# A last batch finished chunk by chunk, and a first attention moved ahead of another batch's transform

## The chip, the cores and the metric

The kernel runs on one core of one Trainium2 chip. The metric is device time in microseconds (us). The traces show five engines of the core: TensorE (PE, matrix products; PEld is its weight load), VectorE (DVE), ScalarE (ACT), GpSimd (POOL) and SyncE (SP, which here only issues transfers). The profile's DMA share is a mean over 16 DMA engines. In this kernel PE writes its results to four PSUM tiles of 128 x 2 x 512 (the two halves are called banks here), and DVE and ACT copy results out of them: 128x512 in 0.69 us on DVE and 0.59 on ACT in the trace of before.

## The reference

```python
def _attn_ref(q, k, v, g_norm):                       # (8, 8, 576, 64) each
    kv = np.einsum('bhsd,bhse->bhde', k, v)
    out = np.einsum('bhsd,bhde->bhse', q, kv)
    rms = np.sqrt(np.mean(out * out, axis=-1, keepdims=True) + 1e-06)
    return (out / rms * g_norm)

def _moe_ref(x, w_proj, filter_fft, w_out):           # x: (8, 576, 512)
    proj = x @ w_proj                                  # 512 -> 3 x 512
    x1, x2, x3 = ...                                   # the three thirds
    X2 = np.fft.rfft(x2, n=S, axis=1)
    H = np.fft.rfft(filter_fft, n=S, axis=0)[None]
    x2_conv = np.fft.irfft(X2 * H, n=S, axis=1)
    return (x1 * x2_conv * x3) @ w_out
```

The output of the attention, its heads side by side, is x of the second function. Everything is float32 outside.

## The kernel before

Both transforms are matrix products with tables of sines. Batches are pipelined: while batch b goes through its transform (`fft`), its gates (`proj13`) and its inverse (`inv`), the attention of batch b + 1 runs (`att_o`, `att_r`, `att_x`), and then its fold (`fold`, the symmetric and antisymmetric parts of x that the projection `proj2` takes). The library that builds the program orders each engine's instructions itself, by readiness and by the order in which they are written; `keep_in_program_order` pins an instruction behind the one written before it on its engine.

```python
    def att_o(b, j):
        ...
        op = ps_tile("ps_o")
        for h in range(2):
            nc.tensor.matmul(op[:, h, 0:TH], kvblk[b % 2][:, j], ...)
        nc.scalar.activation(out=s['sq']..., in_=op[:, :, 0:TH], func=AF.Square)
        if b == 0:
            nc.vector.tensor_scalar_mul(out=o_, in0=op[:, :, 0:TH], scalar1=g_col)
        else:
            nc.scalar.activation(out=o_, in_=op[:, :, 0:TH], func=AF.Copy, scale=g_col)

    def fft(b, g):              # g < 2: two DVE products and a POOL sum; g == 2: one DVE product
        ...
            nc.vector.tensor_mul(out=t_[:n, 0], in0=xp[:n], in1=HH[:n, g, 1:3])
            nc.vector.tensor_mul(out=t_[:n, 1], in0=xp[:n], in1=HH[:n, g, 0:2])
            nc.gpsimd.tensor_add(out=Y[:n, 2 * g:2 * g + 2], in0=t_[:n, :, 0], in1=t_[:n, :, 1])

    def o_rows(b, *blks):       # a block of 64 columns of yg is 64 rows of the output, three apart
        t0 = [SB * (x // 3) + x % 3 for x in blks]
        two = [[(t0[1] - t0[0]) * DM, 2]] if len(t0) == 2 else []
        return bass.AP(tensor=out.tensor, offset=..., ap=[[3 * DM, 64]] + two + [[1, DM]])

    def last(b):
        po = [ps_tile("ps_out") for _ in range(3)]      # five chunks in three PSUM tiles
        ...
        for dc in range(NDC):
            inv(b, (dc,))
            if dc:
                part(dc - 1)                            # a quarter of every chunk
        part(NDC - 1)
        for c in range(NSC):
            ...                                         # copy: ACT for even c, DVE for odd
            for i in range(2):
                (nc.scalar if i else nc.sync).dma_start(out=o_rows(bb, blk), in_=ot[64 * i:64 * i + 64, 0])

    # batch 0's stage in the main loop
            att_o(1, 0); fft(0, 1); att_o(1, 1); att_r(1, 0); fft(0, 0); att_r(1, 1)
            att_x(1, 0); fold(1, 0); att_o(1, 2); proj13(0, 2); att_o(1, 3); att_r(1, 2)
            fft(0, 2); att_r(1, 3); att_x(1, 1); fold(1, 1); proj13(0, 3)
    # later, for every b: outp(b - 1, ...), then last(b) for the last batch, else inv(b, ...)
```

## Time and profile before

| | before |
|---|---|
| time, median of the first 3 runs | 255.63 us (254.88 to 257.65) |
| span of the profiled execution | 252.9 us |
| PE, DVE, ACT, POOL busy | 222.7, 195.1, 153.3, 89.7 us |
| row "43.40 to 61.70": PE idle | 5.2 us |
| row "230.90 to 253.00": PE idle | 10.1 us |
| last copy out of PSUM ends | 249.1 us |

A line of a timeline gives the start, the length, engine, source line, operation, output and input, and in brackets the engine's idle time before it with what ended it. The lines themselves stand in the prediction. The clock in a table by stretches is the one that PE was granted, 1.00 at full speed; the DMA share is the mean busy share of the 16 DMA engines. A run is marked slow when it takes over 1.5% more than the fastest of the same kernel. This line of the page gives the number of output transfers of 256 KB, and the median time from issue to landing:

```profile
out_dram<-ot SPq DMA_DIRECT2D x28, 256.0 KB, 3.6
```

### The profile page before, as it was taken

The numbers are of one execution on the slowest core, as the hardware profiler recorded it, in microseconds if no ns is written. First come the engines' busy times: TensorE is split into PE (matmuls) and PEld (weight loads), VectorE is DVE, ScalarE is ACT, GpSimd is POOL, SyncE is SP. The second block draws the span as 40 slices with busy tenths as digits, with TensorE's granted clock in tenths as the row PEclk, the third lists the DMA queues.
The fourth block names the chain that finished last, engine by engine and source line by source line (L and its number), as shares of the span: only waits on it lengthen the run. The fifth ranks groups of instructions, "written<-read, shape, count | busy, mean of one in ns | idle before, by whom it ended". The sixth has DMA issues, their size and how long they took to land.

```text
span 252.9 us, 4825 instructions
## 1 busy us (share of the span) xinstructions
PE 222.7 (88%) x1927; PEld 132.3 (52%) x1927; DVE 195.1 (77%) x354; ACT 153.3 (61%) x230; POOL 89.7 (35%) x101
## 2 busy tenths in 40 slices
PE   0377997787999999999999999999999999999760
PEld 0343453453665566655665566547664765466420
DVE  6669747799797969795998699769987997696441
ACT  2764336991689468945894689566956696522311
POOL 7964970670491049102920292003300330042000
PEclk9999999999999999999999999999999999999995
DMA  6999999993297529752994199420023003400506
GB/s 69 167 202 251 202 196 191 193 136 43 19 180 85 158 26 181 87 160 54 160 119 115 56 162 118 117 95 1 0 66 103 3 0 75 135 0 3 166 20 187
DMA packets 45623, 27.17 MB, mean 107 GB/s; under 512 B 22274, under 2 KB 40706, under 8 KB 45602
## 3 DMA queue, kind: packets, MB, share of 16 engines
q0 software_dynamic: 40160, 17.44, 55.1%
q1 hardware_dynamic: 5042, 8.78, 12.2%
q10 hardware_dynamic: 400, 0.66, 0.7%
q8 instruction: 15, 0.25, 0.4%
q14 instruction: 6, 0.05, 0.1%
HBM read 33.69 MB, written 9.44 MB: 171 GB/s over the span
## 4 chain that ended last, share of the span: by engine, by line
PE 69%; ACT 13%; DVE 9%; issue 3%; DMA 2%; POOL 2%; ACTq 1%; POOLq 0%; DVEq 0%
PE ps_x L432 19%; PE ps_out L481 10%; PE ps_x L383 6%; PE ps_invo L456 4%; PE ps_inve L456 4%; PE ps_qT L248 3%; ACT lr L284 3%; PE ps_x L389 3%; PE ps_x L374 3%; PE ps_r L283 2%; ACT osb L272 2%; ACT sq L267 2%; DMA vm<-in_v_dram 2%; PE ps_kv L223 2%; PE ps_o L266 2%
## 5 line engine op out<-in xcount | busy, mean ns | idle before, releaser
L432 PE MATMUL ps_x<-x,wp 128*128 128x288 bf16 x512 | 67.8, 286 | 0.7
L415 POOL TENSOR_TENSOR Y<-tpw 128x1024 bf16<-128x1024 f32 (+1 forms) x16 | 37.9, 2366 | 66.3 <-PE ps_r L283 40.7
L432 PEld LDWEIGHTS <-wp 128*128 128x128 bf16 x512 | 49.7, 98 | 15.5 <-issue 2.9
L70 POOL DMA_DIRECT2D km<-in_k_dram x9 | 7.9, 878 | 64.4 <-PE ps_qT L248 58.4
L267 ACT ACTIVATE sq<-ps_o 128x576 bf16<-128x576 f32 x32 | 20.7, 653 | 13.4 <-PE ps_o L266 13.4
L438 DVE TENSOR_TENSOR g<-ps_x,x 128x576 bf16<-128x576 f32 x32 | 24.0, 751 | 5.3 <-PE ps_x L432 3.5
L284 ACT ACTIVATE lr<-ps_r,bias_eps 128x576 f32<-128x576 f32 x32 | 23.5, 751 | 6.9 <-PE ps_r L283 6.9
L436 ACT CAST x<-ps_x 128x576 bf16<-128x576 f32 x32 | 20.7, 648 | 8.4 <-PE ps_x L432 8.4
L481 PE MATMUL ps_out<-wo,yg 128*128 128x512 bf16 x112 | 25.3, 379 | 0.0
L253 DVE COPY qT<-ps_qT 128x512 bf16<-128x512 bf16 (+1 forms) x32 | 13.4, 453 | 14.7 <-PE ps_qT L248 14.6
L456 PEld LDWEIGHTS <-Y 128*128 128x128 bf16 (+1 forms) x192 | 18.2, 97 | 9.2 <-DVE Y L421 1.8
L413 DVE TENSOR_TENSOR tpw<-ps_X,HH 128x1024 f32<-128x1024 f32 (+1 forms) x16 | 19.5, 1219 | 3.9 <-PE ps_X L411 3.3
L272 ACT ACTIVATE osb<-ps_o,g_col 128x576 bf16<-128x576 f32 x28 | 20.9, 746 | 0.0
L248 PE MATMUL ps_qT<-ident,qb 128*64 128x128 bf16 x288 | 12.3, 232 | 9.3 <-DMA qb<-in_q_dram 8.7
L459 ACT COPY os<-ps_invo 128x576 f32<-128x576 f32 x14 | 9.0, 640 | 18.0 <-DVE u L462 15.3
L414 DVE TENSOR_TENSOR tpw<-ps_X,HH 128x1024 f32<-128x1024 f32 (+1 forms) x16 | 19.4, 1213 | 0.0
L287 ACT ACTIVATE rstd<-lr 128x1152 bf16<-128x1152 f32 x16 | 18.6, 1164 | 0.4
L383 PE MATMUL ps_x<-wp,ab 128*128 128x512 bf16 x64 | 16.9, 404 | 1.3 <-DVE ab L312 1.3
L481 PEld LDWEIGHTS <-yg 128*128 128x128 bf16 x112 | 11.0, 98 | 11.9
L492 ACT COPY ot<-ps_out 128x1024 f32<-128x1024 f32 (+1 forms) x10 | 8.8, 885 | 12.9 <-PE ps_out L481 12.9
L266 PE MATMUL ps_o<-qT,kvblk 128*128 128x288 bf16 x64 | 13.8, 304 | 2.9 <-ACT kvblk L234 1.9
L248 PEld LDWEIGHTS <-qb 128*64 128x64 bf16 x288 | 9.6, 117 | 12.3 <-issue 12.3
(166 smaller groups left out, 396.6 us busy)
## 6 DMA issues: line engine op xcount, KB each, us to landing
out_dram<-ot SPq DMA_DIRECT2D x28, 256.0 KB, 3.6
qb<-in_q_dram POOLq DMA_DIRECT2D x16, 288.0 KB, 7.0
km<-in_k_dram POOLq DMA_DIRECT2D x7, 512.0 KB, 6.1
vm<-in_v_dram POOLq DMA_DIRECT2D x7, 512.0 KB, 8.2
wp<-in_moe_w_proj_dram POOLq DMA_DIRECT2D x3, 512.0 KB, 10.1
out_dram<-ot SPq DMA_DIRECT2D x9, 128.0 KB, 3.0
km<-in_k_dram POOLq DMA_DIRECT2D x2, 256.0 KB, 5.5
kt<-in_k_dram POOLq DMA_DIRECT2D x8, 64.0 KB, 5.7
```

Source lines behind the costliest of these rows:

```text
L248: mm = nc.tensor.transpose(tp[64 * hp:64 * hp + 64, bank, i * P:(i + 1) * P], qb[b % 2][:, 2 * jj + hp, c * D:(c + 1) * D], ident)
L267: nc.scalar.activation(out=s['sq'][:, j].rearrange("p (a b) -> p a b", a=2), in_=op[:, :, 0:TH], func=AF.Square)
L272: nc.scalar.activation(out=o_, in_=op[:, :, 0:TH], func=AF.Copy, scale=g_col)
L284: nc.scalar.activation(out=s['lr'][:, j % 2].rearrange("p (a b) -> p a b", a=2), in_=r2[:, :, 0:TH], func=AF.Ln, scale=1.0 / D, bias=bias_eps)
L383: nc.tensor.matmul(pp[:, h], ab[:, j, h * SB:h * SB + P], wp[:, j, DM:2 * DM], start=(j == 0), stop=(j == NDC - 1))
L413: nc.vector.tensor_mul(out=t_[:n, 0], in0=xp[:n], in1=HH[:n, g, 1:3])
L415: nc.gpsimd.tensor_add(out=Y[:n, 2 * g:2 * g + 2], in0=t_[:n, :, 0], in1=t_[:n, :, 1])
L432: nc.tensor.matmul(pp[:, h, 0:TH], w_, x[:, j, h * TH:(h + 1) * TH], start=(j == 0), stop=(j == NDC - 1))
L436: nc.scalar.copy(out=x1, in_=pp[:, :, 0:TH])
L438: nc.vector.tensor_mul(out=st[b]['g13'][:, dc].rearrange("p (a b) -> p a b", a=2), in0=pp[:, :, 0:TH], in1=x1)
L456: nc.tensor.matmul(p_[h][:, i], Y[:n, 2 * g + h, dc * P:(dc + 1) * P], IV[:n, 2 * g + h], start=(g == 0), stop=(g == 2))
L481: nc.tensor.matmul(pp[:, cc], yg[:, dc, c * P:(c + 1) * P], wo[:, dc], start=(dc == 0), stop=(dc == NDC - 1))
```

## The change

Two independent changes were made at once. At the **end**, the inverse of the last batch was to fill in behind and between the halves of batch 6's output projection, and each of the five last chunks got a PSUM tile of its own and one 256 KB transfer from the sync queue. At the **head**, batch 1's attention goes first, with two of its steps moved from ACT to DVE, batch 0's transform products follow, and batch 0's inverse moves into batch 1's stage.

```diff
-            if b == 0:
+            if b < 2:                                   # kvblk, and likewise osb: DVE, not ACT
                 nc.vector.tensor_copy(out=o_, in_=i_)
...
-        mm = nc.tensor.matmul
+        def mm(*a, **kw):
+            i = nc.tensor.matmul(*a, **kw)
+            if b == 0:
+                tc.keep_in_program_order(i)             # likewise the first DVE product
...
+    def out1(b, c, ev, q1):
+        pp = ps_tile("ps_out")
+        ...                                             # all four quarters of chunk c
+        ev(out=ot[:, 0], in_=pp[:, 0])
+        t0 = [...]                                      # first rows of the chunk's two blocks
+        q1.dma_start(out=bass.AP(tensor=out.tensor, offset=out.offset + t0[0] * DM,
+                                 ap=[[(t0[1] - t0[0]) * DM, 2], [3 * DM, 64], [1, DM]]), in_=ot[:, 0])
...
     def last(b):
         for dc in range(NDC):
             inv(b, (dc,))
+            if dc < 2:
+                outp(b - 1, 2 * dc, nc.scalar.copy)
+        for c, ev in ((4, act), (0, dve), (1, act), (2, act), (3, dve)):
+            out1(b, c, ev, nc.sync)
...
+            att_o(1, 0); att_o(1, 1); att_r(1, 0); att_r(1, 1); att_o(1, 2); att_o(1, 3)
+            proj13(0, 2); att_r(1, 2); att_r(1, 3); att_x(1, 0); fold(1, 0); proj13(0, 3)
+            att_x(1, 1); fold(1, 1)
+            for g in (1, 0, 2):
+                fft(0, g)
+            continue
+        if b == 1:
+            for dp in (0, 2):
+                inv(0, (dp, dp + 1))
```

More of the change, by code (lines that the diff above doesn't have):

```diff
@@ L268, in att_o @@
         o_ = s['o'][:, j].rearrange("p (a b) -> p a b", a=2)
-        if b == 0:
+        if b < 2:
             nc.vector.tensor_scalar_mul(out=o_, in0=op[:, :, 0:TH], scalar1=g_col)
@@ L412, in fft @@
             t_ = work.tile([P, 2, 2, DM], FP32, name="tpw", tag="tpw", bufs=2)
-            nc.vector.tensor_mul(out=t_[:n, 0], in0=xp[:n], in1=HH[:n, g, 1:3])
+            i = nc.vector.tensor_mul(out=t_[:n, 0], in0=xp[:n], in1=HH[:n, g, 1:3])
+            if b == 0:
+                tc.keep_in_program_order(i)
             nc.vector.tensor_mul(out=t_[:n, 1], in0=xp[:n], in1=HH[:n, g, 0:2])
@@ L471, in o_rows, with outp @@
         return bass.AP(tensor=out.tensor, offset=out.offset + (b * S + t0[0]) * DM, ap=[[3 * DM, 64]] + two + [[1, DM]])
-    def outp(b, c0):
+    def outp(b, c0, ev=None):
         if c0 < 4 or b % 2:
@@ L488, in outp @@
             n = 2 if c0 < 4 else 1
-            if c0 == 0:
+            if c0 == 0 and not ev:
                 nc.vector.tensor_copy(out=ot, in_=pp)
@@ L497, in outp @@
                     nc.sync.dma_start(out=o_rows(b - 1 + i, NR - 1), in_=ot[64 * i:64 * i + 64, 0])
-    def last(b):
-        po = [ps_tile("ps_out") for _ in range(3)]
-        def part(dc):
-            kw = dict(start=(dc == 0), stop=(dc == NDC - 1))
-            for c in range(4):
-                nc.tensor.matmul(po[c // 2][:, c % 2], st[b]['yg'][:, dc, c * P:(c + 1) * P], wo[:, dc], **kw)
-            for i, y in enumerate((yt[0], st[b]['yg'])):
-                nc.tensor.matmul(po[2][64 * i:64 * i + 64, 0], y[:, dc, 4 * P:S], wo[:, dc], **kw)
+    def out1(b, c, ev, q1):
+        yg = st[b]['yg']
+        pp = ps_tile("ps_out")
+        for dc in range(NDC):
+            kw = dict(start=(dc == 0), stop=(dc == NDC - 1))
+            if c < 4:
+                nc.tensor.matmul(pp[:, 0], yg[:, dc, c * P:(c + 1) * P], wo[:, dc], **kw)
+            else:
+                for i, y in enumerate((yt[0], yg)):
+                    nc.tensor.matmul(pp[64 * i:64 * i + 64, 0], y[:, dc, 4 * P:S], wo[:, dc], **kw)
+        ot = work.tile([P, 2, DM], FP32, name="ot", tag="ot", bufs=3) if c < 3 else \
+            work.tile([P, 2, 2, DM], FP32, name="ot_", tag="tpw", bufs=2)[:, 0]
+        ev(out=ot[:, 0], in_=pp[:, 0])
+        t0 = [x * S + SB * (y // 3) + y % 3 for x, y in (((b, 2 * c), (b, 2 * c + 1)) if c < 4 else ((b - 1, NR - 1), (b, NR - 1)))]
+        q1.dma_start(out=bass.AP(tensor=out.tensor, offset=out.offset + t0[0] * DM,
+                                 ap=[[(t0[1] - t0[0]) * DM, 2], [3 * DM, 64], [1, DM]]), in_=ot[:, 0])
@@ L510, in last @@
+    def last(b):
         for dc in range(NDC):
             inv(b, (dc,))
-            if dc:
-                part(dc - 1)
-        part(NDC - 1)
-        for c in range(NSC):
-            ot = work.tile([P, 2, DM], FP32, name="ot", tag="ot", bufs=3) if c < 3 else \
-                work.tile([P, 2, 2, DM], FP32, name="ot_", tag="tpw", bufs=2)[:, 0]
-            src = po[c // 2][:, c % 2]
-            if c % 2:
-                nc.vector.tensor_copy(out=ot[:, 0], in_=src)
-            else:
-                nc.scalar.copy(out=ot[:, 0], in_=src)
-            for i in range(2):
-                bb, blk = (b, 2 * c + i) if c < 4 else (b - 1 + i, NR - 1)
-                (nc.scalar if i else nc.sync).dma_start(out=o_rows(bb, blk), in_=ot[64 * i:64 * i + 64, 0])
+            if dc < 2:
+                outp(b - 1, 2 * dc, nc.scalar.copy)
+        act, dve = nc.scalar.copy, nc.vector.tensor_copy
+        for c, ev in ((4, act), (0, dve), (1, act), (2, act), (3, dve)):
+            out1(b, c, ev, nc.sync)
@@ L557 @@
             att_o(1, 0)
-            fft(0, 1)
             att_o(1, 1)
             att_r(1, 0)
-            fft(0, 0)
             att_r(1, 1)
+            att_o(1, 2)
+            att_o(1, 3)
+            proj13(0, 2)
+            att_r(1, 2)
+            att_r(1, 3)
             att_x(1, 0)
             fold(1, 0)
-            att_o(1, 2)
-            proj13(0, 2)
-            att_o(1, 3)
-            att_r(1, 2)
-            fft(0, 2)
-            att_r(1, 3)
+            proj13(0, 3)
             att_x(1, 1)
             fold(1, 1)
-            proj13(0, 3)
-        for dc in range(NDC) if b else ():
+            for g in (1, 0, 2):
[4 more added lines that the diff above has]
+                inv(0, (dp, dp + 1))
+        for dc in range(NDC):
             if dc < 3:
@@ L584 @@
                     fold(b + 1, dc // 2)
+        if not nxt:
+            last(b)
+            continue
         if b:
@@ L588 @@
             del st[b - 1]
-        if not nxt:
-            last(b)
-            continue
         for dp in (0, 2):
```

## The prediction

The sum came to 4.2 us for the end, 1.2 for the head and 0.4 on top, 5.8 in all, so 255.6 - 5.8 = 249.8. The 3.6 us for a landing is the median on the page of before. That 1.3 MB within 3 us could cost some tenths (the step from 4.5 to 4.2) and that full PSUM tiles would cost the head 0.5 to 1 were estimates of mine that no trace had shown. Of ACT and DVE on one PSUM tile the trace shows only the times given, 14.37 + 0.65 for the square and 15.05 for the scaling, one after the other.

> **What bounds the kernel now.** I read the page first, then a table by stretches, then the chain of waits for the two stretches that the change touches, then each engine's timeline there.
>
> ```profile
> PE 222.7 (88%) x1927; PEld 132.3 (52%) x1927; DVE 195.1 (77%) x354; ACT 153.3 (61%) x230; POOL 89.7 (35%) x101
> ...
> PE   0377997787999999999999999999999999999760
> ```
>
> TensorE (PE) is at 9 in every slice from the eleventh to the thirty-seventh. The clock is granted in full, so that middle yields nothing to a new order. Holes are only in the first ten slices and the last three (6.3 us each). The table by stretches (length, then busy time of PE, PEld, DVE, ACT, POOL, clock, DMA share, GB/s) puts sizes on them; I cut it at the chain's turns:
>
> ```profile
> 43.40:61.70 18.30, 13.10 (x99) 7.93 (x91) 16.27 (x28) 12.65 (x20) 9.30 (x8) 1.00 1.19 137
> 61.70:86.60 24.90, 24.68 (x229) 15.51 (x230) 21.41 (x38) 17.63 (x26) 9.35 (x8) 1.00 0.69 89
> ...
> 230.90:253.00 22.10, 12.04 (x65) 5.40 (x62) 8.49 (x16) 4.27 (x8) 0.00 (x0) 0.87 0.37 107
> ```
>
> Row one is batch 0's transform with batch 1's attention: 5.2 us of PE idle. Row two is the full stage of batch 1: 0.2 us idle. The last row is the end: 10 us idle. In the chain of waits, row one hangs on ScalarE (ACT) and VectorE (DVE) in turn:
>
> ```profile
> 45.02 0.38 ACT kvblk L234
> ...
> 53.17 1.93 DVE d__646 L304
> ...
> 57.70 0.68 PE ps_invo L456 x4
> ...
> 61.37 0.35 DVE rr L311 x2
> ```
>
> Batch 1's x must be folded before its projection can start, and that fold ends at 61.72; PE takes up the projection at 61.76. In the timeline ACT works from 45.9 to 56.5 without a real gap: 4 squares at about 0.55, 4 scalings (osb) at 0.65, 4 logarithms at 0.67, 2 exponentials at 1.1, 2 copies at 0.55, some 10.8 us. DVE meanwhile takes batch 0's transform products first, then folds.
>
> The end, from the timeline of all engines (start, length, instruction, idle before it):
>
> ```profile
> 244.16 0.59 ACT L522 COPY ot<-ps_out 128x512 f32<-128x512 f32 x1 [2.05 <-PE ps_out L506]
> ...
> 244.78 0.69 DVE L520 COPY ot<-ps_out 128x512 f32<-128x512 f32 x1 [1.32 <-ACT ot L522]
> 246.31 0.59 ACT L522 COPY ot<-ps_out 128x512 f32<-128x512 f32 x1 [1.56 <-DVE ot L520]
> 246.93 0.50 ACTq L525 DMA_DIRECT2D out_dram<-ot  x1
> 247.00 0.69 DVE L520 COPY ot__3269<-ps_out 128x512 f32<-128x512 f32 x1 [1.52 <-ACT ot L522]
> ```
>
> PE's last matmul ends at 244.9. Then five copies run strictly one after another, though two engines share them, because chunks lie pairwise in one PSUM tile. ACT also issues half the transfers between its copies. The last copy ends at 249.1 and the last issue starts at 249.11; transfers there land 2.3 to 2.8 us after issue and the span ends at 252.9.
>
> [...] in batch 0's attention the square of ps_o starts at 14.37, lasts some 0.65, and DVE's scaling of the same tile starts at 15.05. At the end even the two banks of one tile are taken in turn (244.78 after 244.16)[...]; separate tiles should free that. [...] the subtraction d_ took 2.01 us at 53.08, under POOL's addition from 52.30 to 54.66, and 0.55 at 59.75 with POOL idle. [...] for the 256 KB ones the page's median of 3.6 us [...] so I take 3.6.
>
> **The change, part by part.**
>
> *End.* Batch 7's inverse moves from behind the whole of batch 6's output projection to between and behind its halves; the output projection goes chunk by chunk, each in its own PSUM tile, the shared rows first, one 256 KB transfer per chunk from the sync queue. PE's work is the same. From 230.9, when the projections end: inverse piece 0 takes 6 matmuls at 0.124 = 0.75; half of batch 6's output 8 at 0.216 = 1.73; piece 1 0.75; the other half 1.73; pieces 2 and 3 1.5. That is 237.4 without a wait, as Y was done at 229.5 (POOL's second addition starts at 227.12 and takes 2.35) and g at 231.8. Behind each piece come an ACT copy of 0.40 and DVE work of 0.46 + 0.38 + 0.47 = 1.31. ACT also evicts batch 6's halves at 1.0 each; its second ends near 236.9, so the copies of pieces 2 and 3 come at 237.3 and 238.2 (one buffer), and DVE ends piece 3 near 240.0. Before, that was 243.5. PE can meanwhile do three quarters of the first chunks. After 240.0 it has their last quarters (0.34 + 0.22 + 0.22) and two chunks of 0.86: 2.5, so PE ends near 242.5 (before 244.9). The last copy ends near 243.3. Five issues of about 0.65 from 241.0 put the last at 243.6; landing 3.6 makes 247.2, and the 1.2 us that before spends from landing to the end make 248.4. Against 252.9 that is 4.5. The five transfers are 1.3 MB within 3 us, which could cost some tenths: I take **4.2 us**.
>
> *Head.* Batch 1's kvblk and osb go from ACT to DVE, its attention is put ahead of batch 0's products, and batch 0's inverse moves behind batch 1's projection to x2. ACT loses 4 x 0.65 + 0.7 = 3.3 us; kvblk on DVE is ready near 44.9 and not 45.4. ACT then needs 2.2 + 2.7 + 2.2 + 1.1 = 8.2 us from 45.4: rstd is complete near 53.6 instead of 56.5. DVE adds 4 x 0.70 for osb and 0.7 for kvblk, does x (0.75) and the fold (1.95, no POOL addition beside it) for each half, and two g of 0.7. The second half's x starts near 53.7, so the fold ends near **56.4, 5.3 us sooner**. But at that moment PE of before had batch 0's inverse behind it (24 x 0.124 = 3.0 us) and 0.43 of the projection. It leaves 5.3 - 3.0 - 0.4 = 1.9. Also given back: three transform results of batch 0 hold three of the four PSUM tiles until DVE reaches them, and the projection's three tiles must pass through the rest: about 0.5 to 1. That leaves some 1.2.
>
> *DVE as the next limit.* From 43.4 to 86.6 DVE was busy 16.27 + 21.41 = 37.7 of 43.2. Add 3.5, take off 1.5 for the subtraction without POOL: 39.7. With the 1.5 or more that it must wait at the start, batch 2's fold cannot be done much before 84.6, 2.0 sooner than before at best, while both engines depend on each other at over 95% of their time. I take **1.2 us** for the head, likely between 0 and 2.5. Sum: 4.2 + 1.2 = 5.4, and I lean 0.4 above it, because the head's figure counts new stalls in full and none of the 3 to 4 us of DVE slack in each later stage: 5.8. Then 255.6 - 5.8 = 249.8.
>
> **Rivals.**
> (a) DVE becomes the bound of batch 1's stage and eats the whole head. For it: 39.7 of about 41 us, and 5.7 us of products (4 x 1.14 + 1.14) that now begin only after the fold. Against: later stages have DVE at 22 of 26 us, so a backlog that does not gate the fold can be worked off. It would make 251.4 (only the end's 4.2), and 252 with some loss.
> (b) The end stays bound by transfers: five of 256 KB, one queue, each longer than the 128 KB ones. For it: 3.6 against 2.3 to 2.8 us. Against: issues are 0.6 to 0.9 us and the copies come no faster than PE's 0.86 per chunk. If the last landing slips by 1.5 us, the sum is 251.3.
> (c) PE takes the chunks strictly in order and waits for the last piece of the inverse within the first chunk. Then it ends 240.0 + 0.34 + 4 x 0.86 = 243.8, and the gain of the end is 3.3 rather than 4.5: 251.
> (d) The head gains fully: DVE keeps up and the five idle us of row one shrink to two. Then 3 + 4.5 make 248.1.
>
> **Range and chances.** The end is sure in sign, since waits of tile and queue vanish: 3.3 to 4.8. The head is 0 to 3. Together 3.3 to 7.8, so 247.8 to 252.3; I take 247.6 to 252.2 for 8 in 10. 2% is 5.1 us, or 250.5; my middle is 0.7 beyond it with a spread of about 1.8: faster 0.60, same 0.39, slower 0.01.
>
> **What would show each step.** In the new trace: five last copies on ACT and DVE overlapping or 0.86 apart, with no wait of DVE for ACT; PE's last matmul about 6 us before the end of the span instead of 8, and about 11.6 after the last projection instead of 14; batch 1's second fold ending between 55 and 57.5; the d_ subtraction at about 0.55; batch 0's inverse at PE behind the second batch's kv products; PE idle in the stretch that was row one some 3 to 4 us, and new PE waits for DVE in batch 1's stage of at most 1.5. The middle stages should keep 25.3 and 26.4. It goes wrong if PE waits for DVE by 3 us or more in batch 1's stage, if the fold ends after 58, or if the last landing takes well over 4 us.

## The result, and the profile after

The changed kernel takes **274.46 us** (273.7 to 274.95, 4 runs) against 255.25 of before (254.04 to 257.65, 4 runs). The ratio is 1.0737 with a 95% interval of 1.0653 to 1.0821. A ratio here is the mean time of one kernel's fast runs over that of the other's of the same rounds, so it is not quite the ratio of the medians. I had forecast 249.8.

From the page of the changed kernel, its span, its engines, and its rows of 40 slices for PE and the DMA engines:

```profile
span 272.8 us, 4797 instructions
...
PE 219.5 (80%) x1904; PEld 131.7 (48%) x1927; DVE 195.6 (72%) x359; ACT 151.0 (55%) x225; POOL 88.1 (32%) x101
...
PE   0486986879899999999999999999999999980000
...
DMA  7999999954923298519754936001300420141111
```

The last four slices, 27 us, have no work of any engine, and the DMA engines stand at 1: about a tenth. No engine's busy sum has grown by more than 0.5 us. The table by stretches shows that end (length; PE, PEld, DVE, ACT, POOL busy; clock; DMA share; GB/s):

```profile
240.00:245.50 5.50, 4.54 (x19) 1.54 (x19) 3.23 (x7) 1.97 (x4) 0.00 (x0) 1.00 0.39 99
...
250.00:255.00 5.00, 0.00 (x0) 0.00 (x0) 0.00 (x0) 0.00 (x0) 0.00 (x0) 0.50 0.13 52
...
260.00:265.00 5.00, 0.00 (x0) 0.00 (x0) 0.00 (x0) 0.00 (x0) 0.00 (x0) 0.50 0.13 51
```

0.13 of 16 engines is the busy time of two, and they move 51 GB/s between them. The timeline has the last copy and the sync queue's issues:

```profile
244.70 0.69 DVE L518 COPY ot__3271<-ps_out 128x512 f32<-128x512 f32 x1 [0.89 <-PE ps_out L512]
```

```profile
243.45 0.55 SPq L520 DMA_DIRECT2D out_dram<-ot__3239  x1
244.10 9.03 SPq L520 DMA_DIRECT2D out_dram<-ot  x3
253.24 4.94 SPq L520 DMA_DIRECT2D out_dram<-ot__3271  x1
```

Everything is computed by 245.4, where before the last copy ended at 249.1. Then five transfers of 256 KB, 1.31 MB, leave at 51 GB/s, which is 25.7 us by division; the later issues swell too, to between 3.6 and 4.9 us each where the first takes 0.55. In the same trace the four transfers of batch 6, also 256 KB and from the sync queue but with 64 outermost, landed 3.2 to 3.3 us after their issue.

The head changed as well. The chain of waits of the changed kernel, in order of time:

```profile
54.32 0.47 DVE d__701 L304
56.26 0.61 PE ps_x L374 x2
...
58.52 3.56 PE ps_x L383 x8
...
65.25 0.60 PE ps_invo L462 x4
```

The fold is over at 56.2, 5.5 us sooner than before. But the eight matmuls of the projection's second tile then take 3.56 us, and before they took 1.83. The table by stretches says why:

```profile
57.00:58.00 1.00, 0.42 (x4) 0.10 (x1) 1.00 (x2) 0.54 (x1) 0.00 (x0) 1.00 0.26 31
58.00:59.00 1.00, 0.48 (x2) 0.20 (x2) 1.00 (x2) 0.47 (x1) 0.36 (x1) 0.77 0.12 15
...
60.00:61.00 1.00, 1.00 (x3) 0.29 (x2) 1.00 (x2) 0.00 (x0) 1.00 (x2) 0.50 0.00 0
61.00:62.00 1.00, 1.00 (x3) 0.15 (x1) 0.86 (x1) 0.00 (x0) 1.00 (x1) 0.53 0.00 0
```

PE was granted half its clock (0.50) from about 58.5 to 61.9, as the 0.77 and the 0.53 of the rows at both ends give; between 54.8 and 58.5 it had been busy for 1.72 of 3.7 us. What lowered the clock this trace alone doesn't say.

To sum the head, I take the stretch from the fold's end to a common later point, the second group of batch 1's gate projections. For before, then for the changed kernel:

```profile
61.76:71.69 9.93, 9.93 (x128) 5.89 (x129) 8.12 (x12) 6.37 (x10) 4.47 (x6) 1.00 0.42 51
```

```profile
56.26:73.30 17.04, 15.11 (x150) 8.46 (x152) 13.81 (x18) 7.39 (x12) 9.34 (x8) 0.90 0.71 83
```

The stretch grew by 7.11 us: 3.0 for the inverse that moved in, 1.73 for the half clock, 1.93 of PE idle, and 0.45 that I can't assign. With the fold 5.50 sooner and 0.17 more in the rest of the stage, batch 2's projection starts 1.78 us later, at 88.39 and not 86.61. By the last projections the lag is 2.06.

So the difference of the spans, 19.9 us, divides like this: head and middle +2.06; from the last projection to the last copy 12.43 instead of 18.19, -5.76; from the last copy to the end 27.4 instead of 3.8, +23.6.

### The profile page after: what moved, and what is told of

The parts are those of the page before. It is cut to its first block, busy times and chain, and to the rows that moved or that the text cites. A ratio compares the mean times of both kernels' runs of the same rounds, so it can differ in the third digit from the quotient of the medians.

```text
span 272.8 us, 4797 instructions
## 1 busy us (share of the span) xinstructions
PE 219.5 (80%) x1904; PEld 131.7 (48%) x1927; DVE 195.6 (72%) x359; ACT 151.0 (55%) x225; POOL 88.1 (32%) x101
## 4 chain that ended last, share of the span: by engine, by line
PE 58%; DVE 11%; ACT 7%; issue 5%; DMA 5%; POOL 5%; POOLq 0%; DVEq 0%; ACTq 0%
PE ps_x L438 14%; PE ps_out L487 9%; PE ps_x L383 5%; DMA fc<-in_moe_filter_fft_dram,fidx 5%; PE ps_invo L462 4%; PE ps_inve L462 4%; PE ps_X L400 3%; PE ps_qT L248 3%; PE ps_x L389 2%; PE ps_x L374 2%; DVE g L444 2%; PE ps_r L283 2%; ACT lr L284 2%; ACT sq L267 2%; PE ps_x L377 2%
## 5 line engine op out<-in xcount | busy, mean ns | idle before, releaser
L442 ACT CAST x<-ps_x 128x576 bf16<-128x576 f32 x32 | 20.7, 646 | 9.3 <-PE ps_x L438 9.2
L70 POOL DMA_DIRECT2D km<-in_k_dram x9 | 7.9, 881 | 51.5 <-PE ps_qT L248 47.5
L272 ACT ACTIVATE osb<-ps_o,g_col 128x576 bf16<-128x576 f32 x24 | 17.8, 742 | 0.0
L498 ACT COPY ot<-ps_out 128x1024 f32<-128x1024 f32 (+1 forms) x11 | 9.8, 896 | 11.8 <-PE ps_out L487 11.8
L400 PE MATMUL ps_X<-x,FW 128*64 128x512 bf16 (+4 forms) x49 | 15.3, 393 | 0.4
```

The source lines that it names most:

```text
L400: i = nc.tensor.matmul(*a, **kw)
L442: nc.scalar.copy(out=x1, in_=pp[:, :, 0:TH])
```

## The experiments

All kernels gave correct results except the one that says otherwise. Ratios are to the kernel before on the same chip, and of fast runs alone. The medians take in every run: one run of b2 and one of c1 were slow, and without them the medians are 249.5 and 255.26. d1, d2 and d3 ran on another chip than the rest, so they are compared with b2 by ratios.

| run | what it is | median us | ratio (95%) |
|---|---|---|---|
| a1_after_halves | change, last transfers of 64 rows | 253.75 | 0.9993 (0.992 to 1.0067) |
| a2_end_only_halves | old head, new end, 64 rows | 251.13 | 0.989 (0.9817 to 0.9962) |
| a3_head_only | new head, old end | 256.37 | 1.01 (1.0027 to 1.0173) |
| a4_end_only | old head, new end as changed | 272.48 | 1.0747 (1.0657 to 1.0838) |
| b2_end_two_queues | old head, new end, 64 rows, two queues | 250.02 | 0.9812 (0.9756 to 0.9868) |
| b3_end_outer4 | old head, new end, outer dimension 4 | 258.31, one run | wrong |
| c1_third_product_later | a1, one product behind the projection | 255.82 | 1.0042 (0.9968 to 1.0116) |
| c2_products_repeated | a1, extra matmuls in an idle gap | 252.95 | 0.9946 (0.9894 to 0.9998) |
| d1_move_alone | b2 with the move to DVE alone | 253.0 | 0.995 (0.9912 to 0.9987) |
| d2_order_alone | new order without the move, end of b2 | 254.15 | 0.9983 (0.9946 to 1.002) |
| d3_repeated_two_queues | c2 with the end of b2 | 252.16 | 0.9918 (0.9863 to 0.9972) |

My theory after the result was that the access pattern of the last transfers, with its outermost dimension of 2, keeps each on two DMA engines. The rival was that one queue, or the writes themselves, had become the limit. A second question was whether the head loses by itself.

**Transfers of 64 rows (a1).** The amount, the queue and the row order are those of the change.

```diff
-        q1.dma_start(out=bass.AP(..., ap=[[(t0[1] - t0[0]) * DM, 2], [3 * DM, 64], [1, DM]]), in_=ot[:, 0])
+        for i in range(2):
+            q1.dma_start(out=o_rows(bb, blk), in_=ot[64 * i:64 * i + 64, 0])
```

> The changed kernel, but each of the five last 256 KB transfers is split into two of 64 rows, still all from the sync queue. Theory (form: the transfer's outermost dimension of 2 keeps it on 2 of the 16 DMA engines; in the changed kernel's trace 0.13 of the engines' time and 51 GB/s after 245): the 22 us after the last copy shrink to about 5 to 6, total 252 to 254 us, DMA share there over 0.4. Rival (one queue or the writes themselves are the limit: all outputs now leave through one queue): stays above 265 us with the same 51 GB/s.

It took 253.75 us, 20.7 less than the changed kernel. In its trace the DMA share is 0.92 and the rate 208 GB/s in the stretch after the copies, still from the sync queue alone:

```profile
245.00:247.00 2.00, 0.00 (x0) 0.00 (x0) 0.00 (x0) 0.00 (x0) 0.00 (x0) 1.00 0.92 208
```

The rival falls, and what is left of the change is worth nothing against before.

**The end alone, with 64 rows (a2), the head alone (a3), the end alone as changed (a4).**

> The kernel before with the new end alone, transfers in 64-row halves. Theory (the new end is worth what I predicted once the transfers are mended, and the head costs 1.8 us): 249.5 to 251.5 us, about 4 to 5 below before and about 2 below the run with the new head. Rival (the end gains nothing even with mended transfers): within 1 us of before.

> The changed kernel's head with the end of the kernel before. Theory (the head loses 1.8 us between batch 1's fold and batch 2's projection, in a half clock of TensorE and in waits for PSUM): 1.5 to 2.5 us above before, and batch 2's projection starts at 88 to 89 instead of 86.6. Rival (the head is neutral and the 1.8 us came with the new end's other scheduling): within 0.7 us of before.

> The kernel before with the new end alone, its transfers as in the change. Theory (form): 271.5 to 273.5 us, about 2 less than the changed kernel, nearly all of the loss. Rival (head and end interact): more than 4 us from the changed kernel.

a2 took 251.13 us, within what I had written, though it is 3.3 below before rather than 4 to 5. a3 is 2.0 us above before and a4 is 272.48, both within what I had written, except that batch 2's projection starts at 87.43 in a3's trace and not at 88 to 89. The head costs 1% alone (0.3 to 1.7%), and the end's transfers carry nearly the whole loss. The parts add up, since 1.01 for the head and 0.989 for the mended end give 0.9989, and a1 with both measured 0.9993.

**Outer dimension 4 (b3).** Its output is wrong, which doesn't matter for the time. Four of the last five transfers write 128 rows in another order, still as one transfer of 256 KB from the sync queue.

```diff
-                ap=[[(t0[1] - t0[0]) * DM, 2], [3 * DM, 64], [1, DM]]
+                ap=[[X * DM, 4], [s_ * DM, 32], [1, DM]]      # X = 99, s_ = 3; for the fourth chunk 34 and 1
```

> Wrong row order on purpose: the head of before with the new end, where four of the five last transfers stay single 256 KB transfers of 128 rows from sync, but with an outermost dimension of 4 instead of 2 in the access pattern (the fifth is in 64-row halves). Theory (the outermost dimension sets how many of the 16 DMA engines work): the four run at about 100 GB/s, 2.6 us each, DMA share 0.25, and the span ends near 253 to 255. Rival (a single transfer of 128 rows with stepped rows is slow as such, whatever the outer dimension): 51 GB/s as with 2, four times 5.1 us, span over 262.

The table by stretches of this run:

```profile
248.00:250.00 2.00, 0.00 (x0) 0.00 (x0) 0.00 (x0) 0.00 (x0) 0.00 (x0) 0.50 0.26 102
```

Twice the outer dimension gives twice the engines (0.26, 4 of 16) and twice the rate (102 for 51 GB/s). The rate per engine stays at 25.5 GB/s. The span of 256.2 is 1 us longer than I had written. This is the direct evidence for the mechanism, and against the rival that a transfer of 128 stepped rows is slow as such. The 64-row transfers of a1, with 64 outermost, reach a share of 0.92; no other value was run.

**Two queues (b2).** In a2 the sync queue's issues were the next thing to look at. Its timeline:

```profile
239.88 1.13 SPq L515 DMA_DIRECT2D out_dram<-ot__3239  x2
241.10 3.76 SPq L515 DMA_DIRECT2D out_dram<-ot  x6
244.97 1.18 SPq L515 DMA_DIRECT2D out_dram<-ot__3275  x2
```

The last copy ended at 241.8 and the last issues began 3 us later. So the second half of each pair went to ACT's queue and one more copy to DVE.

```diff
-            q1.dma_start(out=o_rows(bb, blk), ...)
+            (nc.scalar if i else q1).dma_start(out=o_rows(bb, blk), ...)
-        for c, ev in ((4, act), (0, dve), (1, act), (2, act), (3, dve)):
+        for c, ev in ((4, act), (0, dve), (1, act), (2, dve), (3, dve)):
```

> The head of before with the new end, 64-row transfers, the second half of each pair issued by ACT instead of sync, and VectorE taking three of the five copies. In the run with all ten on sync, the last copy ended at 241.8 but the last two issues only started at 244.97, because ten issues of 0.56 to 0.62 us follow one another. Theory (the queue's issue time is the next limit of the end): the last issue starts within 0.6 us of the last copy, and the total falls by a further 1.5 to 2.5 us, to 248.5 to 249.8, over 2% below before. Rival (the writes' bandwidth is the limit): within 0.5 us of the run with one queue.

The last issue now begins 0.6 us after the last copy (246.59 after 246.02). The five fast runs have a median of 249.5, within what I had written (250.02 with the slow one), the ratio fell from 0.989 to 0.9812, and it is the fastest kernel here, faster than before beyond noise, but its interval crosses 2%, so the verdict is unclear and not the "over 2%" that I had written. The six runs range from 248.61 to 252.8. The profile is of the slowest of them, which is marked slow, so I use it only to read what happens in such a run. DVE, POOL and PE in it:

```profile
51.21 3.67 DVE L294 TENSOR_TENSOR x<-osb,rstd 128x1152 bf16<-128x1152 bf16 x1 [0.25 <-ACT rstd L287]
```

```profile
51.90 2.36 POOL L415 TENSOR_TENSOR Y<-tpw 97x1024 bf16<-97x1024 f32 x1
```

```profile
55.61 0.66 PE L283 MATMUL ps_r<-sq,ind 128*128 128x288 bf16 x2 [2.48 <-DVE g L438]
56.06 3.41 PE L432 MATMUL ps_x<-x,wp 128*128 128x288 bf16 x16
```

The product x of osb and rstd, 0.75 us at 60.25 in the same trace, takes 3.67 here while POOL's addition runs from 51.90 to 54.26; PE then idles 2.48 us, and its next 16 matmuls take 3.41 us instead of 2.12, at a granted clock of 0.50. The other four traces of this head (before, a2, a4, b3; none slow) show neither: there the same product takes 0.93 to 0.95 us and the clock stays at 1.00 from 50 to 62. Nor is it all of the slow run: its clock was at half from 45.0 to 48.4 as well. So the old head can lose time in this stretch in one run and not in another, and one slow trace doesn't say why.

**The third product later (c1).** Batch 0's third product goes behind batch 1's projection, so that two PSUM tiles and not three wait there for DVE.

```diff
-            for g in (1, 0, 2):
+            for g in (1, 0):
                 fft(0, g)
...
         proj2(b)
+        if b == 1:
+            fft(0, 2)
```

> The changed kernel with 64-row transfers on sync, and batch 0's third transform product put behind batch 1's projection to x2, so that only two PSUM tiles instead of three wait for VectorE there. Theory (the head's loss starts with that PSUM wait of 1.10 us, and the half clock of 3.4 us follows from the idle time around it): no wait for ACT at the second tile of the projection, its 8 matmuls in 1.9 us instead of 3.4, and 2 to 3 us below the run with halves alone (253.75), that is 250.8 to 251.8. Rival (VectorE's backlog in batch 1's stage gates batch 2's fold whatever PE does): less than 0.7 us gained, the waits turn up later in that stage.

My theory failed and the rival held, in that the 2 to 3 us did not come. The ratio is 1.0042 where a1 has 0.9993; the intervals overlap, so c1 is not shown to be slower than a1. The wait at the second tile was gone, but PE waited 0.57 and 1.21 us for DVE's products a little later and 1.10 for ACT behind them, and the half clock came at about 61.2 instead of 58.5.

**Extra matmuls in the gap (c2, d3).** The four matmuls of batch 0's third product run three times over, with the same values, where PE would idle 0.9 us before the projection.

```diff
-        for i, r in enumerate((lo, hi)):
-            mm(xp[r, 0], ...)
+        for _ in range(1 if b else 3):
+            for i, r in enumerate((lo, hi)):
+                mm(xp[r, 0], ...)                       # and the two that complete them
```

> The changed kernel with 64-row transfers on sync; the four matmuls of batch 0's third product run three times over with the same values, which fills TensorE's idle 0.9 us before batch 1's projection and leaves the PSUM wait. Theory (the half clock comes from too little TensorE work in the few us before it): the granted clock stays at 1.00 and the 8 matmuls take 1.9 instead of 3.4 us; 1 to 1.7 us below 253.75. Rival (the clock drops for another reason, or the lost 1.5 us are not on the path): half clock again, or the same time within 0.5 us.

The granted clock stayed at 1.00 here and the eight matmuls took 1.89 us, with the same wait of 1.10 in front of them:

```profile
58.93 1.89 PE L383 MATMUL ps_x<-wp,ab 128*128 128x512 bf16 x8 [1.10 <-ACT x L379]
```

So it was in d3's trace, while all three traces without the repeat (the changed kernel, a1, a3) lost the clock here. That speaks for my theory; d2 below shows that it is not the whole of it. The median fell by 0.8 us only, short of the 1 to 1.7 I had written (by the ratios 1.2, and the intervals overlap): PE now met a wait of 0.64 for POOL's Y that the slow matmuls had covered.

> The whole changed head with batch 0's third product run three times (granted clock stays at 1.00) and the two-queue end. Theory (the end's gain and the head's are separate and add up): as with the one-queue end 1.5 to 2.2 us below that run's 252.95, that is 250.8 to 251.5, still 0.8 to 1.5 us behind the old head with the two-queue end. Rival (with the clock kept, the new head equals the old one): 249.5 to 250.5.

With the better end the whole change takes 252.16 us, a little more than I had written, and 1.1% of before's time behind b2 (0.9918 against 0.9812, the ends of the intervals just touch). So the half clock is a part of the head's loss and probably not all of it. The 1.10, 0.22, 0.18 and 0.29 us that PE waits for ACT and DVE are still in this trace, with 0.62 for POOL.

**The move alone (d1) and the order alone (d2).** These undo one half of the head's change each, with the end of b2. The order includes the pins by `keep_in_program_order` and batch 0's inverse in batch 1's stage.

```diff
 d1: old order;  kvblk and osb of batch 1: if b == 0  ->  if b < 2
 d2: new order;  kvblk and osb of batch 1: if b < 2   ->  if b == 0
```

> The order of before, with the two-queue end, and of the head's change only the move of batch 1's kvblk and osb from ACT to VectorE. Theory (ACT was the chain there, so the move alone shortens it, but VectorE is already taken by batch 0's products): between 1.0 us faster and 0.5 slower than the two-queue end with the old head (250.0). Rival (VectorE is the limit of this stretch and each instruction moved there adds to it): 1.5 to 3 us slower.

> The changed order with the two-queue end, kvblk and osb of batch 1 left on ACT. Theory (the loss of the head comes from the order, from the waits it puts into batch 1's stage): 2 to 4 us slower than the two-queue end with the old head (250.0), as batch 1's fold also ends later than with the move. Rival (the loss comes from the move): within 1 us of 250.0.

d1 took 253.0 us, 1.4% or some 3.5 us behind b2 by the ratios (3.0 by the medians): my theory failed here and the rival held. With the old order the four scalings fall between batch 0's products on DVE; in d1's trace the subtraction d_ also took 2.51 us beside POOL's addition, and PE had half its clock from about 53.4 to 60.2. d2 took 254.15 us, 1.7% or some 4.4 us behind b2 (4.1 by the medians), a little over what I had written; even its two runs with the highest mean clock, 253.23 and 253.74 at 0.996, are over 2 us slower than any fast run of b2. The fold ends at about 58.9 in d2's trace, 2.7 us later than in the changed kernel's; I had predicted 2.9 for taking the two steps off ACT. But d2's trace has PE at half clock from 44.6 to 51.5, which the changed kernel's does not have at all, so the 2.7 us can't be put down to those two steps alone. The order alone costs; that the move wins some of it back rests on d3 (252.16, with the repeat) against d2, since the whole change with this end and without the repeat was not run.

d2's trace also has the same two waits in front of batch 1's projection, and it kept its clock:

```profile
58.92 0.61 PE L374 MATMUL ps_x<-wp,rr 128*128 128x512 bf16 x2 [0.87 <-DVE rr L311]
...
61.18 1.89 PE L383 MATMUL ps_x<-wp,ab 128*128 128x512 bf16 x8 [1.10 <-ACT x L379]
```

Over all 13 traces, between 4 and 236 us, the clock falls to half 12 times, each time for 3.4 us or twice that, and in the 3.4 us before each fall PE had been busy for 1.15 to 1.71 us. So little work goes before every fall but doesn't always bring one: in the changed kernel's trace PE worked 1.06 us between 22.0 and 25.4, and the clock stayed. Several falls lie where the edit of the run changes nothing: c2, d2 and d3 have one from about 24 or 25 to 28, b2 and c1 one from about 45 to 48. So a difference of 1 to 2 us between two single traces can be the clock and not the edit (the one half clock of the changed kernel's trace took 1.73 us).

## Why the prediction was wrong

- **The end's compute: right.** I predicted PE's last matmul 11.6 us behind the last projection and it came 11.6 behind; the last copy was to come 5.8 us sooner against the projections and came 5.76 sooner.
- **The step that failed** is "Five issues of about 0.65 from 241.0 put the last at 243.6; landing 3.6 makes 247.2". The 3.6 us is the median of the 28 transfers on the page of before, of the same 256 KB but with an outermost dimension of 64; I took the size for the shape. The new ones have 2 there, work on 2 of 16 engines (share 0.13) and take 5.1 us each, one after another: 27.4 us from the last copy to the end in place of the 5.1 of my sum. These 22.3 us are most of the 25.7 by which the profiled span of 272.8 exceeds my 247.1 (252.9 less 5.8); the head is nearly all of the rest. a4, with the end alone, confirms it.
- **Rival (b)** named the transfers but made them 1.5 us at most, for size and queue. "The end is sure in sign" was the worst sentence: waits of tile and queue did vanish, and the transfer in their place was never checked. My own sign of going wrong, a last landing of well over 4 us, is what came.
- **The head's fold: right.** 56.4 was predicted and 56.2 measured; 3.3 us of PE idle in the old row one against 3 to 4 predicted; the subtraction at 0.55 as predicted.
- **The head's stalls: mis-sized.** "About 0.5 to 1" for PSUM was 1.10 for the one wait, 1.93 with the smaller ones behind it, and the half clock of 1.73 had no term in the sum. I had also taken off 0.4 for a part of the projection that is done ahead in both kernels. So 1.2 gained became 1.8 lost. Rival (a), DVE in batch 1's stage, was nearest; PE's waits in that stretch name ACT (1.10 and 0.18) and DVE (0.22 and 0.29), and in c2, d2 and d3 POOL's sum as well. Rival (c) did not come, as PE ended when I had said, nor did (d).

Open: the 0.45 us of the head, and why the clock falls in some runs and not in others of the same order. What the interleaved inverse and what the separate PSUM tiles bring at the end was not tested apart. d1 and d2 each bundle several waits, so they don't say how much of the loss is the added DVE time and how much the longer DVE instructions beside POOL's addition (in d1's trace d_ took 2.51 us there and 0.54 at 59.45).

## What to carry to other kernels

Before a transfer is merged or reshaped, look at the outermost dimension of its access pattern (here that of the output in DRAM), not at its bytes alone: here 2 gave a DMA share of 0.13 and 51 GB/s, 4 gave 0.26 and 102, 64 gave 0.92 and 208 with several transfers under way. A share that stays at 0.13, 2 of 16, was the mark of it. Take the landing time for an estimate only from a transfer of the same form. And when work is moved ahead on a chain, count what the engines behind it must now wait for (here 1.93 us of PE idle), and allow for TensorE's clock behind such waits: it stood at 0.50 for 3.4 us in the changed kernel's trace, where eight matmuls took 3.56 us, and in d2's the same eight took 1.89 behind waits of 0.87 and 1.10 us. Before two single traces are compared, look where each of them lost its clock.
